# Two linear-attention and MLP layer pairs: which engine scales the queries in the output stage, and when

## The chip, the cores and the metric

The kernel runs on one core of a Trainium2 chip. The metric is the device time of the whole program in microseconds (us). One core has five engines with instruction queues of their own: TensorE (PE in the profile; PEld is its weight load), VectorE (DVE), ScalarE (ACT), GpSimd (POOL) and SyncE (SP), which here only issues DMA transfers. Engines wait for each other through semaphores. Matrix products are written to PSUM, which this kernel splits into named pools; everything else lives in SBUF or in DRAM.

## The reference

The input x has 2048 tokens of width 576. Four layers are applied, A, B, A, B, each added to its input:

```python
def A(x, wqkv, wo):            # after a layer normalisation; 32 heads of 18
    q, k, v = split(x @ wqkv)
    phi = lambda t: where(t > 0, t + 1, exp(t)) + 1e-6
    pq, pk = phi(q), phi(k)
    kv = einsum("bhsd,bhse->bhde", pk, v)
    z = sum of pk over the tokens
    num = einsum("bhqd,bhde->bhqe", pq, kv)
    den = einsum("bhqd,bhd->bhq", pq, z)[..., None] + 1e-6
    return (num / den) @ wo

def B(x, w1, b1, w2, b2):      # MLP, 576 -> 4608 -> 576, after a layer normalisation
    h = gelu(layernorm(x) @ w1 + b1)
    return h @ w2 + b2

x = x + A(layernorm(x)); x = x + B(layernorm(x))
x = x + A(layernorm(x)); x = x + B(layernorm(x))
```

All weights and the output are bfloat16; the two A layers share their weights, and so do the two B layers.

## The kernel before

Tokens are cut into 16 tiles of 128 (`t`, called tile t below) and four chunks of 512 (`c`), four tiles to a chunk. The 32 heads lie in five groups `g` of 7, 7, 7, 7 and 4 heads, so a group covers 126 rows, the last one 72.

A layer A (`layer_A`, line 324) first walks over the 16 tiles, projects keys and values, and sums `kv` over all tokens. Query projections (`q_proj`, line 363) are mixed in: each makes `pq[(g, c)]`, phi of the queries of one group and one chunk, of 126 (or 72) by 512 elements, with the tokens along the free dimension. There are 20 of them; the last two are done inside the output stage.

The output stage is what the change touches. The division by the denominator is not done on the output: it is folded into `pq`. `den_stage(c)` (line 418) computes the denominators of a chunk on TensorE, takes the reciprocal on VectorE (line 430) and spreads it out with a mask into `quad_rden` (line 432). `scale_stage(g, c)` (line 436) then does three steps for one group: TensorE broadcasts the reciprocals of the group's heads to the group's rows, into PSUM (`rden_ps`, line 438); ScalarE copies that to SBUF as `rden_bc` (line 440); and `pq[(g, c)]` is multiplied by it in place (line 442). This multiplication runs on VectorE, except for the last group of the chunks 1, 2 and 3, where it runs on GpSimd.

`wo_stage(t)` (line 445) makes one output tile: ten products (line 450), two halves of five groups, with `pq[(g, c)]` as weights and `kvwo[g]` (that is kv times wo, made before the loop) as the moving operand, into one of two PSUM accumulators that take turns. So the first half needs the five groups in the order 0 to 4, and a tile needs the accumulator of two tiles before to be free. `residual` (line 309) frees it: VectorE adds the layer's input, `xbf` or `xo` (line 316), and SyncE stores the sum to DRAM (line 321). `prefetch_xo` (line 298) loads the input of a coming tile into one of three buffers (line 301 in the first layer, 304 in the third).

The first four tiles of the stage belong to the MLP's first chunk, and their normalisations (`LNPipe.tick`, line 215) run in this stage: statistics on VectorE (lines 229 to 237), a power on GpSimd (line 242), a product on VectorE (line 246), the normalisation on ScalarE (line 254), a small copy on GpSimd (line 260), then transposes on TensorE (line 267) and their copy on ScalarE (line 269). The MLP's later chunks are loaded back from DRAM (`xl`, line 224) and normalised on VectorE (line 258).

The order of TensorE's instructions in this stage is fixed by hand: `pe()` chains each one behind the one before it, in the order in which the code emits them. On the other engines a scheduler orders the instructions before the run, with the code's order as their priority, and each engine then executes its queue in order. For the loop over the 16 tiles (line 472) the code emits per tile: the prefetches, `wo_stage(t)`, the scaling of groups of the next chunk, a query projection if one is left, at the chunk's third tile `den_stage` of the chunk after the next, and one step of the normalisations. Which groups are scaled at which of the four tiles `j` of a chunk is the tuple in line 481.

Then the MLP begins: `LayerB.run` (line 571), whose first products are those of line 549 and whose second are those of line 596. Its TensorE order is chained too.

Of the kernel before, what the change touches and what calls it, by code (L numbers as in the profile page):

```python
# [20 lines left out]
G = 5  # L21
GH = [7, 7, 7, 7, 4]
GR = [h * DH for h in GH]
# [5 lines left out]
CA = 512  # L29
# [6 lines left out]
def build(tc, A_x, A_wqkv, A_wo, B_w1, B_b1, B_w2, B_b2, out, dbg=None, n_layers=4):  # L36
    nc = tc.nc
    dbg = dbg or {}
    with ExitStack() as ctx:
# [94 lines left out]
        def pe(inst):  # L134
            if pe_chain["on"]:
                if pe_chain["last"] is not None:
                    tc.add_manual_dep(inst.ins, pe_chain["last"], NOSYNC, reason="TensorE order in the MLP")
                pe_chain["last"] = inst.ins.name
            return inst
# [143 lines left out]
        def warm_table(func, after):  # L283
            warm = nc.scalar.activation(out=act_dummy[:, 0:1], in_=neg_half[:, 0:1], func=func)
            tc.add_manual_dep(warm.ins, after, NOSYNC, reason="table of the next stage loaded early")
# [12 lines left out]
        def prefetch_xo(li, t, add_b2):  # L298
            if li == 0:
                xo = work.tile([P, D], BF16, name="xbf", tag="xbf", bufs=3)  # L300
                nc.sync.dma_start(out=xo[:], in_=x_in[t * P:(t + 1) * P, :])
            else:
                xo = work.tile([P, D], F32, name="xo", tag="xo", bufs=3)
                nc.sync.dma_start(out=xo[:], in_=x_d[t])
            if add_b2:
                nc.gpsimd.tensor_tensor(out=xo[:], in0=xo[:], in1=b2_bc[:], op=ALU.add)  # L306
            xo_of[(li, t)] = xo
# [16 lines left out]
        def layer_A(li, next_kind, pre_a1=None):  # L324
# [3 lines left out]
            pq = {}  # L328
# [34 lines left out]
            def q_proj(g, c):  # L363
                qp = ps_h.tile([P, 512], F32, name="q_ps", tag="h")
                for k in range(KD):
                    pe(nc.tensor.matmul(qp[0:GR[g], :], lhsT=wqkv_sb[:, k, GO[g]:GO[g] + GR[g]],  # L366
                                     rhs=yT[:, k, c * CA:(c + 1) * CA],
                                     start=(k == 0), stop=(k == KD - 1)))
                pq[(g, c)] = blk.tile([P, D], BF16, name="pq", tag="blk")
                phi_from_psum(qp[0:GR[g], :], pq[(g, c)][0:GR[g], 0:CA], GR[g], CA)  # L370
# [3 lines left out]
            for t in range(NT):  # L374
# [14 lines left out]
                out=kvT[0:127, 0:4, :].rearrange("p g (h e) -> p g h e", h=7),  # L389
                in0=kvacc[0:127, 0, 0:504].rearrange("p (g h e) -> p g h e", g=4, h=7),  # L390
                in1=maskz[0:127, :, :].unsqueeze(1).to_broadcast([127, 4, 7, DH]), op=ALU.mult)
            nc.vector.tensor_tensor(
                out=kvT[0:127, 4, 0:72].rearrange("p (h e) -> p h e", h=4),
                in0=kvacc[0:127, 1, 0:72].rearrange("p (h e) -> p h e", h=4),
# [23 lines left out]
            def den_stage(c):  # L418
                dp = ps_h.tile([P, 512], F32, name="den_ps", tag="h")
                for g in range(G):  # L420
                    for j in range(TPC):
                        pe(nc.tensor.matmul(dp[32 * j:32 * (j + 1), 0:P], lhsT=zsel[0:GR[g], g, :],
                                         rhs=pq[(g, c)][0:GR[g], j * P:(j + 1) * P],
                                         start=(g == 0), stop=False))
                for j in range(TPC):
                    pe(nc.tensor.matmul(dp[32 * j:32 * (j + 1), 0:P], lhsT=eps_row[:], rhs=one_row[:],
                                        start=False, stop=True))
                rden = work.tile([P, P], BF16, name="rden", bufs=1)
                with nc.allow_low_precision("reciprocal of the denominator in the reference's bfloat16"):
                    nc.vector.reciprocal(out=rden[:], in_=dp[:, 0:P])  # L430
                quad = blk.tile([P, D], BF16, name="quad_rden", tag="blk")
                nc.vector.tensor_tensor(out=quad[:, 0:CA].rearrange("p (j n) -> p j n", j=4), in0=quad_mask[:],
                                        in1=rden[:].unsqueeze(1).to_broadcast([P, 4, P]), op=ALU.mult)
                quad_rden[c] = quad

            def scale_stage(g, c):
                bp = ps_h.tile([P, 512], F32, name="rden_ps", tag="h")
                pe(nc.tensor.matmul(bp[:], lhsT=head_bc[:, g, :], rhs=quad_rden[c][:, 0:CA], start=True, stop=True))
                rb = blk.tile([P, D], BF16, name="rden_bc", tag="blk")
                nc.scalar.copy(out=rb[0:GR[g], 0:CA], in_=bp[0:GR[g], :])  # L440
                eng = nc.gpsimd if c > 0 and g == G - 1 else nc.vector
                eng.tensor_tensor(out=pq[(g, c)][0:GR[g], 0:CA], in0=pq[(g, c)][0:GR[g], 0:CA],  # L442
                                        in1=rb[0:GR[g], 0:CA], op=ALU.mult)

            def wo_stage(t):
                c, j = divmod(t, TPC)
                wp = ps_acc.tile([P, 2, 512], F32, name="wo_ps", tag=("accA", "accB")[t % 2])
                for half in range(2):
                    for g in range(G):
                        pe(nc.tensor.matmul(wp[:, half, 0:HALF], lhsT=pq[(g, c)][0:GR[g], j * P:(j + 1) * P],  # L450
                                              rhs=kvwo[g][0:GR[g], half * HALF:(half + 1) * HALF],
                                              start=(g == 0), stop=(g == G - 1)))
                xn = residual(li, t, wp[:, :, 0:HALF])
                if xn is not None and next_kind == "B" and t < TPC:
                    lnp.feed(xn, t, "B", "act", "act")
# [7 lines left out]
            for g in range(3):  # L463
                scale_stage(g, 0)
            kv_wo(2)
            q_proj(*q_left.pop(0))
            for g in range(3, G):
                scale_stage(g, 0)
# [3 lines left out]
            for t in range(NT):  # L472
                c, j = divmod(t, TPC)
                if j == 0:
                    prefetch_xo(li, t, add_b2=False)
                    prefetch_xo(li, t + 1, add_b2=False)
                elif j < 3:
                    prefetch_xo(li, t + 1, add_b2=False)
                wo_stage(t)
                if c + 1 < NCA:  # L480
                    for g in ((0, 1), (2,), (3,), (4,))[j]:
                        scale_stage(g, c + 1)
                if q_left:
                    q_proj(*q_left.pop(0))
                if j == 2 and c + 2 < NCA:
                    den_stage(c + 2)
                if t == NT - 3:
                    warm_table(ACT.Gelu_apprx_tanh, act_last["exp"])
                lnp.tick()
# [154 lines left out]
        for li, kind in enumerate(kinds):  # L644
            nk = kinds[li + 1] if li + 1 < n_layers else None
            if kind == "A":
                if li == 0:
                    layer_A(li, nk, pre_a1=pre_a1_layer0)
                else:
                    def pre_a1(t):  # L650
                        lnp.tick()
                    layer_A(li, nk, pre_a1=pre_a1)
                while late_pieces:
                    late_pieces.pop(0)()
                while late_pads:
                    late_pads.pop(0)()
            else:
                pe_chain.update(on=True)
                lbs[li].run()
                pe_chain.update(on=False, last=None)  # L660
# [48 lines left out]
```

## Time and profile before

| | us |
|---|---|
| median of 3 runs (lowest to highest) | 812.3 (812.2 to 812.8) |
| the profiled execution, whole | 816.66 |
| its span | 814.7 |
| TensorE busy in the span | 785.2 (96%) |
| ScalarE busy | 352.2 (43%) |
| VectorE busy | 259.2 (32%) |
| GpSimd busy | 120.6 (15%) |
| first output stage, from tile 0's first product to the MLP's first | 91.58 to 128.98 |
| second output stage, the same | 487.54 to 525.94 |

The profiled execution is a single one, with its instructions recorded; its span goes from its first instruction to its last. The granted clock is TensorE's, as a share of full speed; over the whole execution it was 0.989. VectorE's share of the whole span says little about the two output stages, which are 75.8 us of the 814.7: stretches of the span are looked at one by one below.

In a line such as `L442 DVE TENSOR_TENSOR pq<-pq,rden_bc 126x512 bf16<-126x512 bf16 x17`, L442 is the line of the kernel, then come the engine, the operation, what is written from what, the partitions by elements, and the count. In square brackets stands how long the engine had been idle before, and what released it. Waits are given as us in total, times, and the longest.

### The profile page before, as it was taken

Reading aid. Unit: us, or ns where it says so; the run is one execution under the profiler, and the core shown is the slowest. Engines: PE = TensorE matmul, PEld = TensorE weight load, DVE = VectorE, ACT = ScalarE, POOL = GpSimd, SP = SyncE. Lnnn points to the kernel's source line nnn. Section 1 sums busy time; section 2 is a strip of 40 time slices with the busy share of each in tenths; the row PEclk is TensorE's granted clock in tenths of the full one; section 3 lists DMA queues with packets and bytes.
Section 4 is the critical chain, followed back from the end, with each engine's and each line's share of the span. In section 5 each row is a group of like instructions: output and inputs, shape, how many; then the busy total and the mean of one; then the engine's idle time right before and its main releaser. Section 6 shows DMA issues by size and latency. Waiting matters only on the chain.

```text
span 814.7 us, 16146 instructions
## 1 busy us (share of the span) xinstructions
PE 785.2 (96%) x6806; PEld 510.1 (63%) x6812; DVE 259.2 (32%) x764; ACT 352.2 (43%) x765; POOL 120.6 (15%) x218
## 2 busy tenths in 40 slices
PE   5999979999999999999999998799999999999998
PEld 3777554477458647845877765446854774585476
DVE  4675873024303502310345468621400310010000
ACT  4788844610640371066037787274046107403610
POOL 8440131012201201210100002220210110011000
PEclk8999999999999999999999999999999999999999
DMA  9990274002101201100110006820310110011000
GB/s 218 253 327 4 80 230 151 1 31 73 45 25 65 89 1 31 59 31 1 59 60 1 1 1 202 270 83 16 89 43 2 51 57 11 2 44 44 2 23 23
DMA packets 42898, 56.92 MB, mean 70 GB/s; under 512 B 10251, under 2 KB 26891, under 8 KB 42827
## 3 DMA queue, kind: packets, MB, share of 16 engines
q1 hardware_dynamic: 42826, 55.91, 22.6%
q8 instruction: 53, 0.87, 0.4%
q14 instruction: 19, 0.15, 0.1%
HBM read 39.38 MB, written 16.52 MB: 69 GB/s over the span
## 4 chain that ended last, share of the span: by engine, by line
PE 88%; DVE 3%; ACT 3%; DMA 2%; POOL 1%; issue 1%; SPq 0%; DVEq 0%; ACTq 0%
PE m_ps L596 35%; PE h_ps L549 19%; PE hp_ps L549 15%; PE q_ps L366 5%; PE k_ps L336 4%; PE v_ps L347 2%; PE wo_ps L450 2%; PE v_ps L344 2%; PE tp L267 2%; DMA xl<-x_d 1%; PE kvacc L360 1%; DVE xn L316 1%; ACT rden_bc L440 1%; DMA xbf<-in_A_x_dram 1%; POOL ln_rstd L242 1%
## 5 line engine op out<-in xcount | busy, mean ns | idle before, releaser
L596 PE MATMUL m_ps<-w_sb,hT 128*128 128x288 bf16 x2304 | 289.8, 286 | 0.0
L596 PEld LDWEIGHTS <-hT 128*128 128x128 bf16 x2304 | 223.2, 98 | 57.9 <-issue 3.4
L549 PEld LDWEIGHTS <-w_sb 64*128 64x128 bf16 x2304 | 124.4, 94 | 136.5 <-issue 1.7
L549 PE MATMUL hp_ps<-yT,w_sb 64*128 64x512 bf16 x1152 | 178.0, 376 | 0.0
L554 ACT COPY relay_sb<-relay_sb 128x1 f32<-128x1 f32 x144 | 28.5, 198 | 282.4 <-PE h_ps L549 239.4
L549 PE MATMUL h_ps<-yT,w_sb 64*128 64x512 bf16 x1152 | 147.9, 376 | 0.0
L545 ACT ACTIVATE hT<-h_ps,b1T 128x512 bf16<-128x512 f32 x144 | 91.0, 683 | 43.9 <-PE h_ps L549 43.9
L271 DVE COPY yT<-tp 128x640 bf16<-128x640 bf16 x40 | 19.6, 490 | 272.2 <-PE tp L267 272.2
L545 ACT ACTIVATE hT<-hp_ps,b1T 128x512 bf16<-128x512 f32 x144 | 91.1, 692 | 0.0
L242 POOL TENSOR_TENSOR ln_rstd<-ln_u,neg_half 128x1 f32<-128x1 f32 x64 | 35.2, 551 | 339.6 <-DVE ln_u L235 185.6
L306 POOL TENSOR_TENSOR xo<-xo,b_bc 128x576 f32<-128x576 f32 x32 | 40.8, 1275 | 154.1 <-DMA xo<-x_d 152.9
L450 PE MATMUL wo_ps<-kvwo,pq 126*128 126x288 bf16 (+1 forms) x320 | 49.3, 301 | 13.5 <-POOL pq L442 9.4
L549 PE MATMUL h_ps<-yT,w_tail 64*128 64x512 bf16 x144 | 54.1, 376 | 0.0
L549 PE MATMUL hp_ps<-yT,w_tail 64*128 64x512 bf16 x144 | 54.1, 376 | 0.0
L366 PE MATMUL q_ps<-yT,wqkv_sb 128*126 128x512 bf16 (+1 forms) x200 | 50.0, 382 | 0.5 <-ACT phi_a L291 0.5
L450 PEld LDWEIGHTS <-pq 126*128 126x128 bf16 (+1 forms) x320 | 31.7, 102 | 28.5 <-POOL pq L442 10.8
L316 DVE TENSOR_TENSOR xbf<-m_ps,xo 128x576 bf16<-128x576 f32 x16 | 12.1, 757 | 106.9 <-PE m_ps L596 106.9
L336 PE MATMUL k_ps<-wqkv_sb,yT 128*128 128x288 bf16 x320 | 45.9, 291 | 0.0
L289 ACT ACTIVATE phi_e<-k_ps 128x288 bf16<-128x288 f32 x64 | 27.3, 427 | 36.5 <-PE k_ps L336 36.5
L260 POOL COPY y_ring<-y_ring 128x64 bf16<-128x64 bf16 x64 | 15.8, 248 | 158.1 <-DVE y_ring L258 146.2
L292 DVE TENSOR_SCALAR phi_e<-phi_e 128x288 bf16<-128x288 bf16 (+2 forms) x104 | 28.7, 276 | 29.1 <-ACT phi_e L289 28.8
L549 PEld LDWEIGHTS <-w_tail 64*128 64x128 bf16 x288 | 27.1, 94 | 17.1
(94 smaller groups left out, 670.1 us busy)
## 6 DMA issues: line engine op xcount, KB each, us to landing
x_d<-xn SPq DMA_DIRECT2D x48, 288.0 KB, 2.2
xo<-x_d SPq DMA_DIRECT2D x48, 288.0 KB, 3.0
xl<-x_d SPq DMA_DIRECT2D x24, 288.0 KB, 2.9
w_sb<-in_B_w_dram SPq DMA_DIRECT2D x6, 864.0 KB, 9.1
w_sb<-in_B_w_dram SPq DMA_DIRECT2D x9, 512.0 KB, 4.9
x<-in_A_x_dram SPq DMA_DIRECT2D x16, 144.0 KB, 3.8
xbf<-in_A_x_dram SPq DMA_DIRECT2D x16, 144.0 KB, 3.7
out_dram<-xbf SPq DMA_DIRECT2D x16, 144.0 KB, 1.8
```

Source lines behind the costliest of these rows:

```text
L242: nc.gpsimd.tensor_tensor(out=rstd[:], in0=it["u"][:], in1=neg_half[:], op=ALU.pow)
L289: act_last["exp"] = nc.scalar.activation(out=e[0:rows, 0:n], in_=ps_ap, func=ACT.Exp).ins.name
L292: nc.vector.tensor_scalar(out=e[0:rows, 0:n], in0=e[0:rows, 0:n], scalar1=1.0, scalar2=1e-6, op0=ALU.min, op1=ALU.add)
L306: nc.gpsimd.tensor_tensor(out=xo[:], in0=xo[:], in1=b2_bc[:], op=ALU.add)
L316: nc.vector.tensor_tensor(out=xn[:].rearrange("p (h n) -> p h n", h=2), in0=halves, in1=xo[:].rearrange("p (h n) -> p h n", h=2), op=ALU.add)
L336: pe(nc.tensor.matmul(kp[:, 0:HALF], lhsT=yT[:, k, tok], rhs=wqkv_sb[:, k, D + half * HALF: D + (half + 1) * HALF], start=(k == 0), stop=( ...
L366: pe(nc.tensor.matmul(qp[0:GR[g], :], lhsT=wqkv_sb[:, k, GO[g]:GO[g] + GR[g]], rhs=yT[:, k, c * CA:(c + 1) * CA], start=(k == 0), stop=(k ...
L450: pe(nc.tensor.matmul(wp[:, half, 0:HALF], lhsT=pq[(g, c)][0:GR[g], j * P:(j + 1) * P], rhs=kvwo[g][0:GR[g], half * HALF:(half + 1) * HALF ...
L545: act_last["gelu"] = nc.scalar.activation(out=hT[f][:, 0:CB], in_=dst[n], func=ACT.Gelu_apprx_tanh, bias=b1T[:, f:f + 1], scale=1.0).ins.name
L549: mm = pe(nc.tensor.matmul(dst[n], lhsT=wt, rhs=mv, start=(seen[n] == 0), stop=(seen[n] == 8)))
L554: relay = nc.scalar.copy(out=relay_sb[:, 1:2], in_=relay_sb[:, 0:1])
L596: pe(nc.tensor.matmul(acc[:, half, 0:HALF], lhsT=hT[f][:, j * P:(j + 1) * P], rhs=w2_sb[:, f, half * HALF:(half + 1) * HALF], start=(f == ...
```

## The change

The multiplication of line 442 is on VectorE for every group and chunk. And the groups of the next chunk are spread otherwise over the four tiles of a chunk: groups 0 and 1 at the first tile as before, 2 and 3 at the second, 4 at the third, none at the fourth.

```diff
--- before.py
+++ after.py
@@ -438,8 +438,7 @@
                 pe(nc.tensor.matmul(bp[:], lhsT=head_bc[:, g, :], rhs=quad_rden[c][:, 0:CA], start=True, stop=True))
                 rb = blk.tile([P, D], BF16, name="rden_bc", tag="blk")
                 nc.scalar.copy(out=rb[0:GR[g], 0:CA], in_=bp[0:GR[g], :])
-                eng = nc.gpsimd if c > 0 and g == G - 1 else nc.vector
-                eng.tensor_tensor(out=pq[(g, c)][0:GR[g], 0:CA], in0=pq[(g, c)][0:GR[g], 0:CA],
+                nc.vector.tensor_tensor(out=pq[(g, c)][0:GR[g], 0:CA], in0=pq[(g, c)][0:GR[g], 0:CA],
                                         in1=rb[0:GR[g], 0:CA], op=ALU.mult)
 
             def wo_stage(t):
@@ -478,7 +477,7 @@
                     prefetch_xo(li, t + 1, add_b2=False)
                 wo_stage(t)
                 if c + 1 < NCA:
-                    for g in ((0, 1), (2,), (3,), (4,))[j]:
+                    for g in ((0, 1), (2, 3), (4,), ())[j]:
                         scale_stage(g, c + 1)
                 if q_left:
                     q_proj(*q_left.pop(0))
```

## The prediction

> **What bounds the kernel now.** I read the shares of the chain that ended last, then the table of waits, then the busy times by stretch of the two output stages, and last the timeline and the chain inside the first one.
>
> ```profile
> PE 88%; DVE 3%; ACT 3%; DMA 2%; POOL 1%; issue 1%; SPq 0%; DVEq 0%; ACTq 0%
> ...
> PE wo_ps L450 <- POOL pq L442: 9.4, 6, 1.9
> ...
> PE wo_ps L450 <- DVE xn L316: 3.1, 4, 1.1
> ```
>
> TensorE is 88% of the chain, so only time in which TensorE stands still, or runs at a lower clock, can be won. The waits (us in total, times, longest) say that it stood 9.4 us for the scaling done on GpSimd: six times, three per output stage, at tiles 4, 8 and 12. I call these places A, B and C. The next wait on the list is for the residual add on VectorE, which frees the accumulator of two tiles before.
>
> The stage from tile 0's first product to the MLP's first, in stretches that end at tiles 4, 6, 8, about 12, and at the MLP (start:end and length, busy time of PE, PEld, DVE, ACT, POOL, then granted clock, DMA share, GB/s):
>
> ```profile
> 91.58:100.47 8.89, 8.83 (x79) 5.92 (x80) 7.71 (x24) 7.55 (x14) 2.39 (x3) 1.00 0.45 137
> 100.47:108.26 7.79, 5.64 (x35) 3.52 (x34) 5.79 (x16) 5.07 (x9) 5.71 (x10) 0.78 0.78 244
> 108.26:115.41 7.15, 5.76 (x70) 4.09 (x70) 5.45 (x11) 3.54 (x6) 1.15 (x1) 1.00 0.69 204
> 115.41:123.50 8.09, 6.05 (x43) 4.09 (x43) 6.05 (x15) 2.83 (x5) 1.93 (x3) 1.00 0.77 254
> 123.50:128.98 5.48, 4.28 (x33) 2.81 (x31) 4.97 (x14) 0.00 (x0) 1.52 (x4) 1.00 0.71 227
> 91.58:128.98 37.40, 30.57 (x251) 20.43 (x254) 29.97 (x77) 18.99 (x32) 12.69 (x20) 0.95 0.67 211
> ```
>
> TensorE works 30.57 of 37.40 us and VectorE 29.97: there are two nearly equal loads here, and the second takes its instructions strictly in order. The granted clock falls to 0.78 only in the stretch behind A. At A itself:
>
> ```profile
> 100.82 0.36 DVE L442 TENSOR_TENSOR pq<-pq,rden_bc 126x512 bf16<-126x512 bf16 x1
> ...
> 101.59 0.57 ACT L440 CAST rden_bc<-rden_ps 72x512 bf16<-72x512 f32 x1
> ...
> 102.24 1.15 POOL L442 TENSOR_TENSOR pq<-pq,rden_bc 72x512 bf16<-72x512 bf16 x1 [0.25 <-ACT rden_bc L440]
> ...
> 103.44 1.62 PE L450 MATMUL wo_ps<-kvwo,pq 72*128 72x288 bf16 x6 [1.91 <-POOL pq L442]
> ...
> 106.77 1.76 DVE L442 TENSOR_TENSOR pq<-pq,rden_bc 126x512 bf16<-126x512 bf16 x2
> ```
>
> ScalarE copies the last broadcast at 101.59, behind two normalisations; GpSimd multiplies for 1.15; TensorE stands 1.91; and the next six products take 1.62, 0.27 each, where ten take 1.40 (0.14 each) at tiles 1 to 3. The last row is needed below.
>
> The order around these lines isn't the code's. The loads of the MLP's second chunk (line 224) are issued at 110.12, and the Gelu table, which the code warms at tile 13, is loaded at 98.19, between tiles 2 and 3. Instructions are placed into gaps before the run; moving a few can rearrange others. This is the largest uncertainty.
>
> **The change, part by part.** 1. *GpSimd's six multiplications go.* The waits at A, B, C are 1.91, 1.18, 1.26 in the first attention layer and 1.90, 1.19, 1.92 in the second: 9.4. Slow clock behind them: after A, six products 1.62 against 0.84, two broadcasts 1.06 against 0.59, five transposes 0.74 against 0.44, ten products 1.68 against 1.40, in all 1.8; the same in the second layer; behind its C, 36 products in 6.27 against 36 x 0.14 = 5.04, so 1.2. That makes 4.9. The ceiling of the gain is 9.4 + 4.9 = 14.3, if nothing else ended late.
>
> The Trainium skill ("TensorE: Matmul & The Clock Gate", "HAM oscillation — how this bites in real kernels") has TensorE fall to half clock after idle gaps of over about 3.4 us; by that rule gaps of 1.9 cost no clock and the ceiling would be 9.4. The rows here show a clock of 0.78 behind a 1.91 gap, and 1.00 behind gaps of 1.18 and 1.26; I go by the rows.
>
> 2. *Six multiplications come to VectorE*, 0.42 each (two of this 72x512 shape at chunk 0 averaged 422 ns): 2.5. Those at A fall into stretches where VectorE has 7.71 of 8.89 busy; with the third and fourth group also an output tile earlier it is near full. At B and at the first layer's C they disappear in VectorE's own waits for loads (1.39 and 1.32 idle). Without that cover, 0.42 each.
>
> 3. *The broadcasts move by one tile.* Matmul, ScalarE copy (0.58) and multiplication of the last group start after tile 2's or 6's product instead of tile 3's or 7's: one whole product earlier (1.40), plus the denominator stage at A and B. The chain now needs 0.38 + 0.58 + 0.42 = 1.4 with 0.2 of hand-overs, so from tile 3's product (1.40) and four products of the next tile (0.56) it is covered unless ScalarE is late. At A it is late: behind the last exponential stand the table load (1.28) and its dummy (0.20). There the last group inherits the place that the fourth has now, whose multiplication starts at 100.82; one more broadcast matmul in front adds 0.22, so it ends near 101.4, needed near 101.0: 0.4 of 1.9 stays. Two broadcasts back to back at tile 1 need two of three PSUM buffers; ScalarE returned the earlier pair by 94.34, ahead of 95.6. No DMA is moved by the code itself; SyncE's order may shift only with the residual adds that its stores wait for.
>
> 4. *What is late next, at A.* VectorE. From 101.4 stand before tile 4's residual: quad 0.43, statistics 0.45, tile 3's residual 0.75, and a further statistics set (about 1.5): 104.5, against 105.16 now. Then two multiplications (0.8) and tile 5's residual near 106.0 to 106.7, against 108.46 and, in the second layer, the counterpart of 107.96. TensorE alone could start tile 6 at 105.7 instead of 108.26. So A is worth between 0.7 (only tile 4's residual) and 2.5 (TensorE's own pace); I take 1.5, from tile 5's residual, whose store goes ahead of the next load. Two layers: 3.0.
>
> 5. *At B.* The stretch behind it hangs on a load, not on GpSimd (start, length, in the chain):
>
> ```profile
> 110.12 4.18 DMA xl<-x_d
> ...
> 114.33 0.46 DVE ln_st L229
> ...
> 115.66 0.56 POOL ln_rstd L242
> ...
> 116.99 0.75 DVE xn L316
> ```
>
> A normalisation of the MLP's next chunk stands in VectorE's queue before tile 8's residual, and waits for its load; tile 10's product then waits for that residual until 117.80. If this order stays, B's 1.2 only becomes a longer wait at tile 10, perhaps with slow clock. I take 0, bounds -0.9 (half of A's clock loss) and +1.2 per layer.
>
> 6. *At C.* In the first layer tile 11's residual waits for a load issued at 118.14 that takes 4.63: 0, bounds 0 and 1.26. In the second the chain does run through GpSimd's 1.12 into 36 products; but tile 13 also needs tile 11's residual, which VectorE began at 519.98 after 8.18 busy us of 9.24. It ended at 520.72, just when tile 13 started. I take the stretched normalisation there (1.15 beside GpSimd, 0.58 elsewhere: 0.57 won) less 0.42: 0.15, bounds -0.4 and 3.1 (1.92 + 1.2).
>
> 7. *Contention.* The last row at A: a multiplication of 0.4 took 1.36 while GpSimd did an add of 1.27 (106.57). It is the only one of VectorE's 34 stretched so.
>
> A rule against the change stands in the Trainium skill ("SBUF — State Buffer", "Who interferes with whom"): a VectorE instruction with two SBUF inputs and a GpSimd one that reads SBUF block each other for the whole of an instruction. Were all six new ones hit by the remaining adds, that would be 6 x 0.94 = 5.6 lost; the trace has one case in 34, so the sum takes 0.
>
> Sum: 3.0 + 0 + 0.15 = about 3.2 us won. The profiled execution took 816.66 (span 814.7 and 2.0 around it), 4.4 or 0.5% above the median of 812.3; the saving is a difference inside the span, and I take it from the median: **809.1**, its own range from the bounds at A and small order effects 806.5 to 811.
>
> **The rivals.** *The queues close up.* If tile 8's residual is placed ahead of the normalisation, and C follows, most of TensorE's waits come out: A 2.5 twice, B 1.2 twice, half of the second C's 3.1 make 9.0, less a fifth for multiplications on a full VectorE: 7.5, so 804.8. For it: the placement reacts to TensorE being earlier. Against: DMA share already 0.67 to 0.78, loads of 4 us.
>
> *A load moves further ahead in VectorE's queue (slower).* With its earlier work done sooner, VectorE has a gap before tile 6 or 7, and the normalisation of the next chunk is placed one tile earlier, before a residual that TensorE needs. Its load lands no sooner, so the present wait of 1.39 grows by one tile's pace (37.40/16 = 2.3) to 3.7 per layer; both layers 7.4, less A's 3.0: 4.4 slower, 816.7. It decides from 1.5 per layer on, where it eats A. For it: 1.39 and 1.75 waited at this very place now. Against: the load can't be placed before its tile's store.
>
> *VectorE is the bound and nothing changes.* A's 3.0 against six times 0.42: 0.5 won, 811.8. For it: 100% busy in the first 3 us behind A. Against: 7.4 us idle in the stage.
>
> **How the numbers follow.** Chances: forecast 0.42, queues close up 0.20, load ahead 0.26, nothing 0.12. A difference under 0.2% (1.6 us) can't be told from none in this kernel. Of the forecast's case 0.03 lies over 810.7; so faster 0.59, same 0.15, slower 0.26. The range goes from 803, below the second case's time by a part of its uncertainty, to 817, which holds half of the slower case.
>
> **What would show it.** Right: no wait of TensorE for GpSimd; under 0.7 of wait at tile 4; clock near 1.00 behind A; MLP starts 1 to 2.5 us earlier in each layer; wait for the residual add above 3.1. Wrong: at tile 8 a shorter wait for the load (second case), or VectorE waiting over 3 us for line 224's loads (third). If TensorE still stands over 1 us at tile 4, now for VectorE, step 3 is wrong.

## The result, and the profile after

| | before | after |
|---|---|---|
| median of 8 runs each, us (lowest to highest) | 813.07 (812.2 to 815.15) | 808.0 (807.11 to 810.64) |
| the profiled execution, whole | 816.66 | 807.19 |
| its span | 814.7 | 805.2 |
| first output stage | 37.40 | 33.55 |
| second output stage | 38.40 | 34.18 |

The ratio of after to before is 0.993, with a 95% interval of 0.9913 to 0.9947: faster by 5.1 us, where 3.2 were forecast. The two profiled executions differ by more, 9.5 us of span. Of these, 3.85 and 4.22 lie in the two output stages. The other 1.4 lie in front of the first one, in a part that the edit does not touch: TensorE's busy time there is 80.12 us in before and 79.05 in after, with a granted clock of 0.72 and 0.86 between 8 and 20 us, and its idle time is 0.4 shorter in after. A second profiled execution of before, taken with the experiments, took 816.14 with stages of 36.81 and 38.13. So both profiled executions of before lie above its medians, and what the profiles show place by place is somewhat more than what the medians give.

The shares of the chain that ended last, then TensorE's waits (us in total, times, longest), after:

```profile
PE 89%; DMA 4%; DVE 4%; ACT 1%; issue 1%; SPq 1%; POOL 1%; DVEq 0%; POOLq 0%; ACTq 0%
```

```profile
PE wo_ps L449 <- DVE xn L316: 6.5, 6, 2.3
...
PE wo_ps L449 <- DVE pq L441: 1.1, 1, 1.1
```

The 9.4 us of waiting for GpSimd's multiplication are gone, and no row for it is left. The wait for the residual add, 3.1 before, is 6.5 now: about a third of what was taken away comes back there. The waits for the multiplication and for the residual add together were 12.5 and are 7.6 now, 4.9 us less.

Busy times by stretch: the two whole stages (the first row starts 0.04 before tile 0), the 7.0 us behind tile 4's start in the first, and the end of the second (columns as before: start:end, length, busy PE, PEld, DVE, ACT, POOL, granted clock, DMA share, GB/s):

```profile
90.10:123.69 33.59, 28.95 (x251) 19.87 (x254) 28.13 (x72) 18.78 (x32) 9.25 (x15) 1.00 0.70 223
482.26:516.44 34.18, 30.18 (x250) 20.50 (x253) 27.28 (x72) 18.57 (x32) 5.10 (x12) 0.95 0.75 251
98.98:106.00 7.02, 5.73 (x46) 3.83 (x45) 6.59 (x18) 5.04 (x9) 4.26 (x6) 1.00 0.79 245
510.80:516.44 5.64, 5.46 (x30) 3.48 (x30) 2.23 (x3) 0.00 (x0) 0.00 (x0) 0.70 0.86 286
```

The gain in the first stage divides in two. TensorE's busy time fell from 30.57 to 28.95 at the same number of products: 1.6 us of slow clock gone, since the clock behind tile 4 is 1.00 where it was 0.78. The rest, 2.2, is less standing still. In the second stage the clock is not whole: it is 0.70 behind the last long wait.

Where along the stage the lead is won shows when the start of each tile's products is set against tile 0's (us, worked out from the timelines; first stage, then second):

| tile | before | after | lead of after |
|---|---|---|---|
| 4 | 8.9, 8.9 | 8.9, 8.9 | 0, 0 |
| 5 | 14.7, 14.7 | 12.4, 11.4 | 2.3, 3.3 |
| 7 | 19.1, 19.1 | 18.0, 15.9 | 1.0, 3.2 |
| 8 | 20.8, 20.8 | 19.6, 17.6 | 1.2, 3.2 |
| 9 | 23.8, 23.8 | 21.3, 19.3 | 2.6, 4.6 |
| 10 | 26.2, 26.6 | 23.1, 22.2 | 3.1, 4.4 |
| 12 | 29.3, 29.6 | 25.8, 24.9 | 3.5, 4.8 |
| 13 | 32.1, 33.6 | 27.5, 28.6 | 4.6, 5.0 |
| MLP | 37.40, 38.40 | 33.55, 34.18 | 3.85, 4.22 |

Tile 5 begins only when tile 4's six last products are done, so a wait at tile 4 shows at tile 5, and likewise at 9 and 13. The leads are taken before rounding. A wins 2.3 and 3.3, of which 1.2 is lost again at tile 7 in the first stage only. B wins 1.3 and 1.4 at tile 9, and up to tile 12 another 1.0 and 0.2 follow. C wins 1.1 and 0.2, and behind tile 13 about 0.8 is given back in each stage.

The timeline at A in the first stage, after (start, length, engine and line, operation; idle time and releaser in brackets):

```profile
97.59 1.28 POOL L306 TENSOR_TENSOR xo<-xo,b_bc 128x576 f32<-128x576 f32 x1 [2.07 <-DMA xo<-x_d]
...
98.37 0.56 ACT L440 CAST rden_bc<-rden_ps 72x512 bf16<-72x512 f32 x1
...
99.41 0.21 DVE L246 TENSOR_SCALAR ln_nmr<-ln_mv,ln_rstd 128x1 f32<-128x1 f32 x1 [1.02 <-POOL ln_rstd L242]
99.54 0.95 DVE L430 RECIPROCAL rden<-den_ps 128x128 bf16<-128x128 f32 x1
...
100.41 0.36 DVE L441 TENSOR_TENSOR pq<-pq,rden_bc 72x512 bf16<-72x512 bf16 x1
...
100.82 0.91 PE L449 MATMUL wo_ps<-kvwo,pq 72*128 72x288 bf16 x6 [1.15 <-DVE pq L441]
...
101.74 0.74 DVE L316 TENSOR_TENSOR xn<-wo_ps,xbf 128x576 f32<-128x576 f32 x1
...
102.51 0.70 DVE L316 TENSOR_TENSOR xn<-wo_ps,xbf 128x576 f32<-128x576 f32 x1
...
103.19 0.45 DVE L229 BATCH_NORM_STATS2 ln_st<-xn 128x6 f32<-128x288 f32 x1
...
104.92 1.27 POOL L306 TENSOR_TENSOR xo<-xo,b_bc 128x576 f32<-128x576 f32 x1
...
105.10 1.37 DVE L441 TENSOR_TENSOR pq<-pq,rden_bc 126x512 bf16<-126x512 bf16 x1
...
108.18 1.39 PE L449 MATMUL wo_ps<-kvwo,pq 126*128 126x288 bf16 x10 [0.83 <-DVE xn L316]
```

The copy of the last broadcast ends at 98.93, but its multiplication runs at 100.41, because two instructions stand in front of it on VectorE: one that waits 1.02 for GpSimd's power, which GpSimd could only do after an add of 1.28, and then a reciprocal of 0.95. TensorE still stands 1.15, now for VectorE. (In the second stage no add stands in front of the power there, and TensorE stands 0.13.) The six products take 0.91, at full clock. Then tile 4's residual (102.51) comes directly behind tile 3's and ahead of tile 3's statistics. At 105.10 a multiplication is stretched to 1.37 beside GpSimd's add, and tile 7 starts only at 108.18, with 0.83 of wait for a residual that was queued behind it. Before has one such multiplication too, in the last row at A in the prediction.

### The profile page after: what moved, and what is told of

Read it like the earlier page. It is cut to its first block, busy times and chain, and to the rows that moved or that the text cites. A ratio compares the mean times of both kernels' runs of the same rounds, so it can differ in the third digit from the quotient of the medians.

```text
span 805.2 us, 16152 instructions
## 1 busy us (share of the span) xinstructions
PE 780.9 (97%) x6806; PEld 508.4 (63%) x6812; DVE 261.0 (32%) x770; ACT 351.2 (44%) x765; POOL 114.8 (14%) x212
## 4 chain that ended last, share of the span: by engine, by line
PE 89%; DMA 4%; DVE 4%; ACT 1%; issue 1%; SPq 1%; POOL 1%; DVEq 0%; POOLq 0%; ACTq 0%
PE m_ps L595 35%; PE h_ps L548 19%; PE hp_ps L548 15%; PE k_ps L336 4%; PE q_ps L366 4%; PE v_ps L347 3%; PE v_ps L344 2%; PE tp L267 2%; PE wo_ps L449 2%; DMA xo<-x_d 1%; DMA x<-in_A_x_dram 1%; DVE xn L316 1%; PE kvacc L360 1%; DMA xbf<-in_A_x_dram 1%; ACT rden_bc L440 1%
## 5 line engine op out<-in xcount | busy, mean ns | idle before, releaser
L271 DVE COPY yT<-tp 128x640 bf16<-128x640 bf16 x40 | 19.6, 490 | 266.8 <-PE tp L267 266.8
L449 PE MATMUL wo_ps<-kvwo,pq 126*128 126x288 bf16 (+1 forms) x320 | 45.8, 292 | 8.7 <-DVE xn L316 6.5
```

## The experiments

Each ratio is against runs of before on the same chip, whose medians were 814.85 (the first four experiments), 814.71 and 815.11. The diffs are against after where nothing else is said. Two theories stand against each other. One: the gain comes from starting the broadcasts a tile earlier, above all at A, and the engine hardly matters. The rival: it comes from VectorE's faster multiplication. A second question is how much the work that does not belong to the stage takes: the loads and normalisations of the MLP's next chunk, and GpSimd's adds for the MLP.

**1. The engine alone.** All scaling on VectorE, the groups at their old tiles.

```diff
-                    for g in ((0, 1), (2, 3), (4,), ())[j]:
+                    for g in ((0, 1), (2,), (3,), (4,))[j]:
```

> All scaling on VectorE, but the groups stay at the tiles where they were before. Theory (the earlier start carries most of it, because the last group's broadcast then has a whole output tile more of cover): the multiplication gets 0.7 us shorter, but starts behind the same ScalarE copy, so TensorE still waits about 1.2 us at tile 4 and 0.4 to 0.5 at tiles 8 and 12; gain over before 1 to 2.5 us (810.5 to 812). Rival 'slow GpSimd is all': as fast as the change, about 808. Rival 'the queues rearranged themselves': anything, following where the loads of line 224 stand.

815.71; ratio 1.0006 (0.9987 to 1.0024): no gain at all, where 1 to 2.5 us were expected. TensorE's waits in this kernel:

```profile
PE wo_ps L449 <- DVE pq L441: 6.6, 6, 2.6
...
PE wo_ps L449 <- DVE xn L316: 3.9, 3, 1.6
...
PE wo_ps L449 <- DVE ln_u L237: 3.0, 2, 1.5
```

The six waits for GpSimd have become waits for VectorE: 6.6, and 3.0 more that the trace puts on the instruction beside it. What VectorE does at tile 8 in this kernel shows why (timeline):

```profile
111.51 0.46 DVE L229 BATCH_NORM_STATS2 ln_st<-xl 128x6 f32<-128x288 f32 x1 [0.57 <-DMA xl<-x_d]
111.88 0.40 DVE L441 TENSOR_TENSOR pq<-pq,rden_bc 72x512 bf16<-72x512 bf16 x1
...
112.34 0.91 PE L449 MATMUL wo_ps<-kvwo,pq 72*128 72x288 bf16 x6 [1.63 <-DVE pq L441]
```

The last broadcast was copied by 110.61, and the multiplication takes 0.40 in place of GpSimd's 1.15, but it stands behind statistics that wait for a load. What the faster engine saves, its queue takes.

**2. The move alone.** The groups early as in after, the last group of chunks 1 to 3 on GpSimd as in before.

```diff
-                nc.vector.tensor_tensor(out=pq[(g, c)][0:GR[g], 0:CA], in0=pq[(g, c)][0:GR[g], 0:CA],
+                eng = nc.gpsimd if c > 0 and g == G - 1 else nc.vector
+                eng.tensor_tensor(out=pq[(g, c)][0:GR[g], 0:CA], in0=pq[(g, c)][0:GR[g], 0:CA],
```

> Groups one tile earlier, but the last group of chunks 1 to 3 is still multiplied on GpSimd. Theory: 0.38 + 0.58 + 1.15 and hand-overs are 2.3 us, against a cover of one product (1.40), four products (0.56) and at tiles 4 and 8 the denominators (0.56); TensorE's waits for GpSimd fall from 9.4 us to under 3, gain 2.5 to 5 us, that is 808 to 810.5. Rival 'slow GpSimd is all': same as before, 813, waits for GpSimd over 6 us.

811.19; ratio 0.9942 (0.9919 to 0.9965). The interval overlaps that of after and not that of the engine alone. One row of its waits:

```profile
PE wo_ps L450 <- POOL pq L442: 1.7, 4, 0.8
```

With GpSimd still multiplying, its wait falls from 9.4 to 1.7, and the time lies a little above the expected 808 to 810.5. Of the two theories the first holds and the rival falls. A third reading, that each of these edits gained or lost by what it rearranged in the queues, is what the next two experiments are for.

**3. After, with the foreign work held back.** The loads of line 224 for the MLP's second chunk and the loads behind GpSimd's first adds (line 304) are issued only after the stage's last store.

```diff
+                        if it["load"] < 2 * TPC:
+                            tc.add_manual_dep(ld.ins, last_store[it["after"]], NOSYNC, reason="load after the stage's last store")
...
+                if add_b2 and t < TPC:
+                    tc.add_manual_dep(ld.ins, last_store[li - 1], NOSYNC, reason="load after the stage's last store")
```

> The changed kernel, with the loads of the next MLP chunk (line 224) and of the MLP's first residual inputs issued only after the output stage's last store, so no foreign normalisation and no GpSimd add stands in the stage. Theory (behind the change VectorE's queue, filled with the next chunk's normalisations, and the loads set the stage): the remaining waits of TensorE for the residual add, 6.5 us in the changed kernel, fall under 2, the stage gets 2 to 4 us shorter twice, 802 to 805. Rival 'the stage is bound by TensorE and the residual's own loads': no gain, 807 to 809, since xbf and xo still arrive late. Rival 'the work is only put off': the MLP's second chunk waits for its normalisations, 808 or more.

**4. Before, with the same held back.** The same edit in before.

> The kernel before with the same loads held back. With e4 it gives the change's effect without rearranged normalisations. Theory: TensorE's waits for GpSimd remain (9 us and the slow clock behind tile 4), so e4 is faster than this one by 6 us or more, more than the 5 us between the two originals. Rival 'the change gained by the order of the loads in VectorE's queue': e4 and e5 are equal within 2 us, and e5 is at 808 or below.

After with holding: 804.48, ratio 0.9853 (0.9828 to 0.9878). Before with holding: 809.04, ratio 0.9902 (0.9878 to 0.9927). One row of TensorE's waits of each, the first from after with holding, the second from before with holding:

```profile
PE wo_ps L456 <- DVE xn L321: 4.0, 3, 1.6
```

```profile
PE wo_ps L457 <- POOL pq L449: 9.0, 6, 1.9
```

After with holding lies in its expected 802 to 805, but TensorE's wait for the residual add fell to 4.0 and not under 2. Holding alone is worth 5.8 us in before and leaves its waits for GpSimd untouched (9.0). On top of it the change is worth 4.6, about as much as without (each interval reaches some 2 us to either side). The theory had said at least 6 and the rival at most 2; neither number was met. By these numbers the two savings add up: the change removes waits for the scaling, holding removes waits behind foreign work. Engine and move were not tried one by one with the foreign work held.

**5. Only chunk 1's broadcasts early (A).** All on VectorE.

```diff
-                    for g in ((0, 1), (2, 3), (4,), ())[j]:
+                    for g in (((0, 1), (2, 3), (4,), ()) if c == 0 else ((0, 1), (2,), (3,), (4,)))[j]:
```

> All scaling on VectorE, but only chunk 1's groups are a tile earlier, so only the wait at tile 4 (place A) gets its cover; tiles 8 and 12 are as in the run with the engine alone, which was no faster than before. Prediction's split (A is worth nearly all, 3.0 of 3.2): 809 to 811, about the change's own time. Rival 'tiles 8 and 12 carry at least half': 811.5 to 814.

**6. Only the chunks 2 and 3 early (B and C).** The same line with `c > 0`.

> The complement: all scaling on VectorE, chunk 1's groups at their old tiles, chunks 2 and 3 a tile earlier. Prediction's split: no faster than before, 813 to 815 with the wait at tile 4 kept. Rival 'tiles 8 and 12 carry at least half': 809 to 812.

A alone: 808.8, ratio 0.992 (0.9898 to 0.9943), as good as after. B and C alone: 812.3, ratio 0.9966 (0.9949 to 0.9984), between the prediction's split (813 to 815) and the rival's 809 to 812. The interval leaves out 1, so B and C are worth something by themselves. Against the engine alone (815.71) A's move is worth 6.9 and that of B and C 3.4; together they would make 10.3, and all three moved make 0.76% by the ratios, 6.2. So by the middle values they do not add up, and whoever moves A has what B and C would bring; the excess of 4.1 is not far above the scatter, since each interval reaches 1.4 to 1.8 us to either side. The second stages of the traces show how that can be. With A alone TensorE waits 0.73 and 2.17 there for the scaling at tiles 8 and 12; after waits 1.09 and 2.33 for residuals at tiles 10 and 13 instead, and the MLP begins 34.28 and 34.18 us into the stage. In the first stages the two profiled executions differ (36.16 and 33.55), so why the medians are alike was not settled.

**7. Before again.** No edit, for the scatter.

> The kernel before once more, for a second profile: the first one's execution lay 3.6 us above the median. If the difference of the two first profiles (9.5 us in the span, 8.0 in the two stages) is partly that execution, this one's two stages together are 1 to 3 us shorter than 75.8; if they are 75.8 within 0.5, the rest of the difference lies elsewhere.

814.26, ratio 0.9983 (0.9963 to 1.0004). The two stages of its profiled execution make 74.9 us, 0.9 less than 75.8, which lies between the two cases expected. Single runs of before lay between 809.4 and 819.4 over the three chips; effects under about 2 us between two experiments are not told apart here.

**8 and 9. The order of a residual put back.** In after, tile 4's residual pinned behind tile 3's statistics, where before has it; and, in another kernel, tile 8's residual pinned behind the normalisation of the MLP's next chunk, as in before.

```diff
+            if li % 2 == 0 and t == 4:
+                tc.add_manual_dep(add.ins, u_last[3], NOSYNC, reason="residual behind the statistics")
```

```diff
+                            if it["load"] == 4:
+                                tc.add_manual_dep(res8.pop(), yi.ins.name, NOSYNC, reason="residual behind the normalisation")
```

> The changed kernel, but tile 4's residual stands in VectorE's queue behind the statistics of tile 3, as it did before the change (in the changed kernel it was placed in front of them). The prediction's step 4 assumed this old order and took 1.5 us per layer for it. If that working was right and the new order made the rest, this run is 1.5 to 3 us slower than the change: 809.5 to 811. Rival 'the order there doesn't matter, the broadcasts' start does': 808 within 0.8.

> The changed kernel, but tile 8's residual stands behind the whole normalisation of tile 4 of the next MLP chunk, as before the change. The prediction's step 5 took this order and so 0 for place B. If B's 1.2 to 1.4 us per stage (from the start times of tile 9) came from the new order, this run is 1.5 to 3 us slower than the change: 809.5 to 811. Rival 'the load, issued 2 us earlier, is what helped': 808 within 0.8, and VectorE doesn't wait for the load.

Tile 4's: 811.47, ratio 0.9953 (0.9929 to 0.9978). Tile 6 then starts 1.4 and 0.4 us later than in after (first stage, second), and 0.3 and 0.2 of that are left at tile 8. Tile 8's: 811.48, ratio 0.9962 (0.9944 to 0.998); tile 10 starts 1.5 later in the first stage and at the same time in the second. By the ratios the two kernels are 1.9 and 2.6 us slower than after, but both intervals overlap its interval, and in both kernels tile 13 of the first stage starts some 4 us later than in after (31.4 and 31.7 against 27.5). There VectorE waits for loads that the pin has rearranged. With tile 4's residual pinned it is a load of line 224 (timeline):

```profile
122.73 0.46 DVE L229 BATCH_NORM_STATS2 ln_st<-xl 128x6 f32<-128x288 f32 x1 [3.82 <-DMA xl<-x_d]
123.11 0.74 DVE L318 TENSOR_TENSOR xn<-wo_ps,xbf 128x576 f32<-128x576 f32 x1
...
123.90 5.28 PE L453 MATMUL wo_ps<-kvwo,pq 126*128 126x288 bf16 x30 [3.88 <-DVE xn L318]
```

A load of the foreign work in front of a residual thus cost TensorE 3.88 here, which is what the prediction's slower rival describes. The local effect of each order is shown by the timelines; its share of the whole time stays open.

**10 and 11. Which of the held loads counts.** After, with only the loads of line 224 held; after, with only the loads for GpSimd's adds held (one of the two conditions of experiment 3 each).

> The changed kernel with only the next chunk's normalisation loads (line 224) held behind the stage's last store; GpSimd's adds for the MLP's residuals stay in the stage. If the normalisations in VectorE's queue are what the stage still waits for, most of the 3.6 us of the run that held both: 804.5 to 806, with one or two multiplications still stretched to 1.4 us. If GpSimd's adds are: 807 to 808.

> The complement: the changed kernel with only the loads for GpSimd's adds held behind the stage's last store; the normalisations stay. No multiplication over 0.5 us. If contention with GpSimd and these loads matter: 805 to 806.5; if the normalisations do: 807 to 808.

805.5, ratio 0.9887 (0.9862 to 0.9913), and 807.13, ratio 0.9904 (0.9881 to 0.9926). Both lie where the normalisations were said to weigh more than the adds (804.5 to 806, and 807 to 808). Beyond after's 0.993 that is 0.43% and 0.26%, and both together gave 0.77%: by the middle values they add up, though the first interval touches that of after and the second overlaps it. With the normalisations held, two multiplications are still stretched, to 1.36 and 1.10. With the adds held, the multiplication that took 1.37 in after looks like this (timeline; three multiplications in a row):

```profile
104.32 0.40 DVE L446 TENSOR_TENSOR pq<-pq,rden_bc 126x512 bf16<-126x512 bf16 x1
...
104.76 0.37 DVE L446 TENSOR_TENSOR pq<-pq,rden_bc 126x512 bf16<-126x512 bf16 x1
...
105.23 0.41 DVE L446 TENSOR_TENSOR pq<-pq,rden_bc 126x512 bf16<-126x512 bf16 x1
```

No multiplication takes over 0.43 there. Tile 5 of the first stage starts 11.4 us after tile 0 instead of 12.4, since GpSimd's power for the third tile no longer stands behind an add, and tile 7 starts at 15.9 instead of 18.0. So the adds cost 1.0 us at A and 1.1 more up to tile 7, by the stretched multiplication and a power that waits behind an add, and 1.3 of that reached the MLP's start.

**12. After with holding, and the last group's multiplication ahead of the reciprocal.** On top of experiment 3, the reciprocal of the chunks 2 and 3 is chained behind the last group's multiplication, which removes what stood in front of it in the timeline at A.

```diff
+                    rc = nc.vector.reciprocal(out=rden[:], in_=dp[:, 0:P])
+                    if c > 1:
+                        tc.add_manual_dep(rc.ins, last_mult["n"], NOSYNC, reason="last group scaled first")
```

> The kernel with the held loads (804.5), and the reciprocals of chunks 2 and 3 placed behind the last group's multiplication in VectorE's queue. Theory (the rest of the wait at tile 4 is the 0.95 us reciprocal in front of it): another 0.4 to 1 us per stage, 803 to 804. Rival 'covered, or given back at the next residual': 804.5 within 0.7.

803.05, ratio 0.9846 (0.982 to 0.9872): the fastest of all, 1.5% under before. Over experiment 3 it gains 0.07% by the ratios, 0.6 us, and the intervals overlap, so that last step is not shown. Nor does its trace show the wait gone: in experiment 3 hardly any was left at tile 4 (tile 5 starts at 11.4, as in after's second stage), and here TensorE waits 0.97 at the next chunk's broadcast instead, so tile 5 starts 12.2 us into both stages.

## Why the prediction was right, and where it was not

The direction was right, and 808.0 lies in the range; the gain was 5.1 where 3.2 were forecast. It lies between the forecast and the rival "the queues close up" (804.8; its own sum, 9.0 less a fifth, would be 7.2 and not 7.5). Of the signs set down, the waits for GpSimd, the clock behind A and the longer wait for the residual add came as the forecast has them. The MLP's start did not: it came 3.85 and 4.22 us earlier, not 1 to 2.5. And the sign of the second case came too, a shorter wait for the load at tile 8 (none and 0.39 us, against 1.39 and 1.75). The steps one by one:

- *Steps 1 and 2, the price of what goes and comes.* The waits for GpSimd went, and six more multiplications on VectorE did not make it the bound. The slow clock behind A went with the gap, as the rows had said: 1.6 us of TensorE's busy time in each stage, against 1.8 counted behind A.
- *Step 3, the move.* It is the effective part, as experiments 1 and 2 show: without it the change of engine brings nothing. The prediction worked out the move and the engine in one chain and did not say this. The wait left at A was put at 0.4; it was 1.15 in the first stage and 0.13 in the second. ScalarE's copy, named there as the late one, was done at 98.93; late was VectorE, behind a GpSimd power that stood behind a GpSimd add. By the prediction's own test (over 1 us at tile 4) this step fails in the first stage.
- *Step 4, A's worth.* Taken as 1.5 per stage with bounds of 0.7 and 2.5; at tile 8 it was 1.2 and 3.2. The assumed order (statistics and a second set of them before tile 4's residual, at 104.5, which is 12.9 us into the stage) did not come: the residual ran 12.4 us into it, at 102.51. In the second stage nothing took the gain back; in the first the stretched multiplication did. In experiment 5 A's broadcasts alone were enough for the whole gain, by the middle values, and experiment 8 shows that the residual's place moves tile 6.
- *Step 5, B at 0.* This is the term that was furthest off: 1.3 and 1.4 were won at tile 9, above the bound of 1.2, and 3.5 - 1.2 = 2.3 and 4.8 - 3.2 = 1.6 up to tile 12. It rested on "if this order stays", and the order did not stay. These are the rows around tile 8, after:

```profile
106.52 0.33 SPq L224 DMA_DIRECT2D xl<-x_d  x1
...
110.85 0.45 DVE L229 BATCH_NORM_STATS2 ln_st<-xl 128x6 f32<-128x288 f32 x1
...
112.41 0.75 DVE L316 TENSOR_TENSOR xn<-wo_ps,xbf 128x576 f32<-128x576 f32 x1
```

  The load goes out 16.4 us into the stage instead of 18.5, so the statistics begin without a wait (a wait of 1.39 before), and the residual of tile 8 runs ahead of the normalisation's last steps. In the second stage the load goes out 14.3 instead of 18.05 us into the stage. That is the mechanism of the rival "the queues close up"; it came true at B but not at the second stage's C. Experiment 9 puts the order back and parts the two: in the first stage tile 10 loses 1.5, so the order counts there; in the second it loses nothing (TensorE waits 1.05 for the residual at tile 10, 1.09 in after, 1.14 in before), so there the earlier load carries the gain. The opposite, a load that moves ahead and stalls VectorE, did not happen in after, although the load did move ahead: its data came earlier too. It did happen in experiment 8.
- *Step 6, C.* In the second stage right: 0.15 taken, 0.2 won (4.8 of lead at tile 12, 5.0 at tile 13). One reading behind it was off: tile 13 did not begin just when tile 11's residual ended, at 520.72, but at 521.10, because the six products before it ran at half clock. These are the residual and the products that wait for it (timeline of after, end of the second stage):

```profile
510.04 0.75 DVE L316 TENSOR_TENSOR xn<-wo_ps,xo 128x576 f32<-128x576 f32 x1
...
510.84 2.03 PE L449 MATMUL wo_ps<-kvwo,pq 126*128 126x288 bf16 x11 [2.33 <-DVE xn L316]
```

  The 1.92 for GpSimd has become 2.33 for the residual, and the slow clock stayed, from 512.00 on (rows in the last section). In the first stage tile 13 has 1.1 more lead than tile 12, within the bounds of 0 and 1.26, where 0 was taken.
- *Step 7, contention, taken as 0.* Again one multiplication was stretched, to 1.37 (and one to 0.61), and about 1.1 us were lost there; the adds' second effect, the late power at A, was not in the list at all. The rule in the Trainium skill ("SBUF — State Buffer", "Who interferes with whom"), that a VectorE instruction with two SBUF inputs and a GpSimd one that reads SBUF shut each other out, agrees with the rows and with experiment 11, which takes the adds away. It was no reason against the change, since before had the same collision once, but the price should have stood in the sum.

In sum, by the traces the stages won 8.1 where 3.2 was summed: A 4.45 at tile 8, where 3.0 stood; B 2.65 at tile 9, where 0 stood; 1.15 more between tiles 9 and 12; 1.3 at C, where 0.15 stood; and 1.5 given back at the end of the stages. The terms were taken well below their upper bounds; these, 5.0 for A, 2.4 for B and 1.26 for the first stage's C, make 8.7, near what the traces show (single values, 3.2 at A and 1.3 and 1.4 at B, lie above theirs). So the mechanism at A was right in the main, its size and B's were not, and that the median's gain of 5.1 lies so near 3.2 is partly luck. What stays open is why the profiled executions differ by 9.5 where the medians differ by 5.1; no profile of an execution near the median of before was taken. The clock may be a part of it: the profiled execution of after had a mean granted clock of 0.996, the highest of its eight runs (the others 0.992 to 0.994), and that of before had 0.989.

## What to carry to other kernels

Putting a late step on a faster engine gave nothing here, because that engine's queue had other work in front of it; starting the step earlier did, even on the slow engine. Where instructions are placed before the run, a small move reorders loads and adds elsewhere, so a term of 0 that rests on "the order stays" should be weighed against the gain of the other order. And look in the stage's queues for work that is not the stage's own: holding it back was worth as much here (5.8 us) as the change (5.1).

## What the runs showed of the hardware

The clock does not follow the length of a gap alone. Two kernels have nearly the same gap at the same place, the end of the second stage. First after, where the residual's wait of 2.33 ends at 510.84 (stretches with busy times and granted clock, columns as before):

```profile
508.50:510.80 2.30, 0.01 (x1) 0.00 (x0) 1.59 (x4) 0.00 (x0) 0.99 (x3) 1.00 0.89 300
510.84:512.00 1.16, 1.16 (x10) 0.92 (x10) 0.34 (x1) 0.00 (x0) 0.00 (x0) 1.00 0.62 238
512.00:515.00 3.00, 2.87 (x13) 1.67 (x12) 1.14 (x2) 0.00 (x0) 0.00 (x0) 0.50 0.94 317
```

Then after with the adds held, where a wait of 2.34 ends at 511.46:

```profile
508.50:511.50 3.00, 0.66 (x7) 0.40 (x5) 2.17 (x6) 0.00 (x0) 1.01 (x3) 1.00 0.87 285
511.50:513.50 2.00, 1.56 (x12) 1.12 (x12) 1.02 (x2) 0.00 (x0) 0.00 (x0) 1.00 0.77 240
513.50:515.50 2.00, 2.00 (x18) 1.55 (x17) 0.94 (x2) 0.00 (x0) 0.00 (x0) 1.00 0.90 346
```

In the one the clock falls to 0.50, more than a microsecond after the products have begun again; in the other it never falls. That is part of why the second kernel's stage is 32.95 long and the first's 34.18. The Trainium skill ("TensorE: Matmul & The Clock Gate", "HAM oscillation — how this bites in real kernels") warns of gaps over about 3.4 us. The runs differ: gaps of 1.9 to 2.3 can bring the fall, or not; behind the gaps of 1.50 and 1.63 of experiment 1 six products took 0.91, full speed, and behind gaps of 1.50 in experiment 6 the clock fell to 0.50 in both stages.

The clock records of the fourteen traces show what decides. In each execution the clock changes only at marks 3.413 us apart: before's falls begin at 103.40, 499.35 and 519.83, which is 116 and then 6 times 3.413 apart, and each lasts 3.41. Between two marks of after, 508.59 and 512.00, lie 2.26 of its gap, and the clock falls at the second mark. With the adds held a mark at 510.59 cuts the gap in two, 1.47 before it and 0.87 behind, and the clock does not fall. Counted over all traces, without their first 16 and last 10 us: all 18 stretches between marks in which TensorE stood idle for over 1.8 us, more than half, were followed by a fall; of the four with 1.7 to 1.8, two; of more than 3000 with less, one (1.39, in experiment 10). So two near gaps can add up: 1.56 and 1.33, seen at the same place with both loads held, put 2.02 of idle time between the marks at 503.23 and 506.64, and the clock fell at the second.

The marks lie elsewhere in each execution (in the traces the first fall to 0.50 begins between 10.6 and 13.7 us). A forecast of slow clock behind one gap of about 2 us, as in the prediction's step 1, should so be a chance, not a certainty.
